# One two-run mask product per bank of transposed scores

## The chip, the cores and the metric

The kernel runs on one core of one Trainium2 chip. The metric is the device time of one execution in microseconds (us): median 1925.46 of three runs, 1924.97 to 1925.52.

## The reference

One transformer block on x of 2048 rows by 576, in float32: an adaptive layer norm, sliding-window attention with 32 heads of 18 channels, a second adaptive layer norm, a token mixer and an MLP. The change is in the attention, where row i sees row j if 0 <= i - j < 256:

```
h = _layernorm(x) * (1 + ca) + sa
scores = einsum("bhqd,bhkd->bhqk", q, k) * (Dh ** -0.5)
mask = (idx[:, None] - idx[None, :] >= 0) & (idx[:, None] - idx[None, :] < W)   # W = 256
p = softmax(where(mask, scores, -1e9))
o = einsum("bhqk,bhkd->bhqd", p, v)
x = x + ga * (o @ wo)
```

## The kernel before

The kernel has four stages in one program: projections to q, k and v (`qkv`), attention with the output projection woven in (`attention`), the mixer and the MLP. The order of all instructions is written out by hand: every step is entered with a due time by `at(t, f)`, `build` sorts the steps by that time and issues them, and each engine then works through its own list in that order. Buffers are given by tags; an instruction that takes a buffer waits until the last reader of the one before it is done.

**Units of attention.** The 2048 rows are four groups of 512 queries (g = 0 to 3). Within a group, `load(n)`, `qs`, `ks`, `mx` and `xm` run over n = 0 to 31, with g = n // 8. This text calls an n a head, though it holds four heads of the reference: two passes j = 0, 1, each over a pair of heads that lies side by side in the partitions. Scores are computed twice. First, `mx` makes them with queries in the partitions, in blocks of 64 queries, two blocks to a call (`bb` = 0 to 3); a product with the identity adds the mask (L450, L452), VectorE takes the maximum of each row (`red`, L460), TensorE transposes the maxima of a head (`mtr`, L468), ScalarE copies them (L472), and SP stores them as extra rows of the query tile (`mst`, L477). Second, two heads later, `xm` makes the scores again, transposed, with keys in the partitions and the maxima subtracted by the extra rows; `ex` (L522) takes their exponential on ScalarE, and `av` (L544) multiplies by the values.

**The transposed scores.** A pass has twelve blocks of 64 keys, b = -4 to 7 (group 0 has none below 0). Block b meets the queries `rng(b)`, at most 320 columns. `BANKS` (L479) packs the blocks into five PSUM banks of 512 columns: for example bank 0 holds block 0 at column 0 and block 5 at column 320. Banks take the tags s0 and s1 in turn, so a bank's first product waits for the exponential of two banks before. In each block the first 64 columns (the diagonal) and the last 64 (the window's far edge) may need a mask of 64 x 64, repeated for the two heads of the pass: `Mk[:, 1]` for the diagonal, `Mk[:, 0]` for the far edge. Each holds 0 or -1e30.

**The edited step.** `xm` issues the one to three score products of a bank (L492) and then its masks. It lists the columns that need a mask (`mk`), joins a far edge with the diagonal that begins just behind it into one run of 128 columns, and issues one product `identr` x `Mk` for each run (L517): the stationary operand is the identity, the moving operand the mask, and the result is added in PSUM. Where a bank has two runs of 128, it issues instead one product for the far edges of both and one for the diagonals of both, each with an output of two runs of 64 (L504 to L513). Every bank except number 4 so has two mask products, and bank 4 has one. The widths are 64 + 128 columns for banks 0 and 1 and 128 + 128 for banks 2 and 3 in groups 1 to 3; in group 0 they are 64 + 128, 64 + 64, 64 + 128, 64 + 128 and, for bank 4, 64. Both operands of every product are float32r, and each product has its own weight load.

**What shares the engines.** Between the steps of attention the schedule puts the output projection of finished rows (`wotile`): loads, transposes to T (L608, L610, copied at L615 to L618), the products (L629), the residual (L633), two layer norms (L116 to L122, L642, L643, L652) and stores. PSUM tags m0 and m1 belong to `mx`, s2 and s3 to the value products, the transposes and the projection. The query tiles have four buffers and the key tiles three; POOL makes the masked copies `QS` (L431) and `KS` (L438).

**Set-up.** `consts` clears `zb`, makes the identity and its float32r copy; `masks` clears `Mq` and `Mk`, fills them by four selections on POOL, and copies the lower 64 partitions to the upper 64 on VectorE (L103). `zb` serves only `warm`, which nothing calls.

Of the kernel before, what the change touches and what calls it, by code (L numbers as in the profile page):

```python
# [6 lines left out]

F32 = mybir.dt.float32
F32R = mybir.dt.float32r
BF16 = mybir.dt.bfloat16  # L10
# [8 lines left out]
P = 128  # L19
# [12 lines left out]
class Kern:  # L32
# [8 lines left out]
    def setup(self, stack):  # L41
        nc, tc = self.nc, self.tc
        self.ev = []
        self.cst = stack.enter_context(tc.tile_pool(name="cst", bufs=1))
        self.dr = stack.enter_context(tc.tile_pool(name="dr", bufs=1, space=DRAM))
        self.ps = stack.enter_context(tc.tile_pool(name="psU", bufs=1, space=PSUM))
        self.pools = {}
        c = self.cst
        self.zb = c.tile([P, P], BF16, name="zb")
        self.ident = c.tile([P, P], F32, name="ident")  # L50
        self.identr = c.tile([P, P], F32R, name="identr")
        self.gb = c.tile([P, D], F32, name="gb")
        self.mhalf = c.tile([P, 1], F32, name="mhalf")
        self.rowm = c.tile([P, 8], F32, name="rowm")
        self.Mq = c.tile([P, 2, 64], F32R, name="Mq")
        self.Mk = c.tile([P, 2, 64], F32R, name="Mk")
        self.md = c.tile([P, 10], F32, name="md")
        self.qd = [self.dr.tile([2, D, 512], F32, name=f"qd{g}") for g in range(4)]
        self.kd = [self.dr.tile([2, D, 768], F32, name=f"kd{g}") for g in range(4)]
        self.vd = [self.dr.tile([P, VW], F32, name=f"vd{t}") for t in range(NT)]  # L60
        self.od = [self.dr.tile([512, D], F32, name=f"od{g}") for g in range(4)]
        self.xp = [self.dr.tile([P, D], F32, name=f"xp{t}") for t in range(NT)]
        self.hbd = [self.dr.tile([P, D], F32, name=f"hbd{t}") for t in range(NT)]
        self.xnd = [self.dr.tile([P, D], F32, name=f"xnd{t}") for t in range(NT)]
        self.modd = {v: self.dr.tile([1, D], F32, name=f"modd{v}") for v in (2, 3, 4, 5)}

    def at(self, t, f, *a):
        self.ev.append((t, (lambda: f(*a)) if a else f))
# [14 lines left out]
    def consts(self):  # L83
        nc = self.nc
        g = nc.gpsimd
        g.memset(self.zb, 0.0)
        make_identity(nc, self.ident)
        nc.vector.tensor_copy(self.identr, self.ident)
        g.memset(self.mhalf, -0.5)

    def masks(self):
        nc = self.nc
        g = nc.gpsimd
        for M in (self.Mq, self.Mk):
            g.memset(M.bitcast(F32), 0.0)
        h = slice(0, 64)
        sel = lambda t, s, op, cm: g.affine_select(out=t, in_=t.bitcast(F32), pattern=[[s, 64]], compare_op=op, fill=NEG, base=0, channel_multiplier=cm)
        sel(self.Mq[h, 0], 1, ALU.is_gt, -1)
        sel(self.Mq[h, 1], -1, ALU.is_ge, 1)
        sel(self.Mk[h, 0], -1, ALU.is_gt, 1)  # L100
        sel(self.Mk[h, 1], 1, ALU.is_ge, -1)
        for M in (self.Mq, self.Mk):
            nc.vector.tensor_copy(M[64:128], M[0:64].bitcast(F32))  # L103
        m = self.rowm
        v = self.ident[:, 0:108].rearrange("p (u r d) -> p u r d", u=3, r=2)
        for r in range(2):
            nc.vector.tensor_reduce(out=m[:, r:r + 1], in_=v[:, :, r, :], axis=mybir.AxisListType.XY, op=ALU.add)
        nc.vector.tensor_tensor(out=m[:, 2:4], in0=m[:, 0:2], in1=self.ident[:, 108:110], op=ALU.add)
        nc.vector.tensor_reduce(out=m[:, 4:5], in_=self.ident[:, 108:110], axis=mybir.AxisListType.X, op=ALU.add)
# [17 lines left out]
    def qkv(self, T0, TB):  # L127
        nc, at, ps = self.nc, self.at, self.ps
# [189 lines left out]
        def vst(t):  # L318
            nc.sync.dma_start(self.vd[t], X["Vst"][t % 3])

        def warm(n):
            pw = ps.tile([P, 512], F32, tag="m0", name="pw")
            for _ in range(n):
                nc.tensor.matmul(pw, self.zb, self.zb.unsqueeze(1).to_broadcast([P, 4, P]), start=True, stop=True)

        at(-90, cond)
        for i in range(2):
            at(-89 + i, xload, i)
# [21 lines left out]
        for b in range(4):  # L350
# [7 lines left out]
            for i in range(4):  # L358
                t = 4 * b + i
# [16 lines left out]
            if b < 3:  # L376
                for i in range(4):
                    t = 4 * b + 4 + i
# [13 lines left out]
    def attention(self, t1, t2, TA, HU, LX=2.05):  # L392
        nc, at, ps = self.nc, self.at, self.ps
        X, M = {}, self.rowm
# [86 lines left out]
        def rng(b):  # L481
            return max(0, 64 * b), min(512, 64 * b + 320)

        def xm(n, j, k):
            g = n // 8
            px = X["px", n, j, k] = ps.tile([P, 512], F32, tag=f"s{(5 * j + k) % 2}", name=f"X{n}_{j}_{k}")
            Q, K = X["Q"][n % 4], X["ks", n, j]
            blocks = [x for x in BANKS[k] if g or x[0] >= 0]
            mk = []
            for i, (b, c) in enumerate(blocks):  # L490
                q0, q1 = rng(b)
                nc.tensor.matmul(px[:, c:c + q1 - q0], K[:, b + 4].rearrange("p r k -> p (r k)"), Q[:, j, q0:q1], start=(i == 0), stop=False)  # L492
                if b >= 0:
                    mk.append((c, 1))
                if b <= 3:
                    mk.append((c + q1 - q0 - 64, 0))
            mk.sort()
            runs = []
            for c, kind in mk:
                if kind == 1 and runs and runs[-1] == (c - 64, 64, 0):  # L500
                    runs[-1] = (c - 64, 128, 0)
                else:
                    runs.append((c, 64, kind))
            if len(runs) == 2 and runs[0][1] == 128 and runs[1][1] == 128:  # L504
                d = runs[1][0] - runs[0][0]
                c = runs[0][0]
                out = px[:, c:c + 128]
                o2 = px.rearrange("p (a b) -> p a b", b=64)
                a0, da = c // 64, d // 64
                for h in range(2):  # L510
                    pass
                full = [(o2[:, a0 + h:a0 + h + da + 1:da, :], self.Mk[:, h].unsqueeze(1).to_broadcast([P, 2, 64])) for h in range(2)]
                ops = full  # L513
            else:
                ops = [(px[:, c:c + w], self.Mk.rearrange("p a b -> p (a b)")[:, 64 * kind:64 * kind + w]) for c, w, kind in runs]
            for i, (o, mv) in enumerate(ops):
                nc.tensor.matmul(o, self.identr, mv, start=False, stop=(i == len(ops) - 1))  # L517

        def ex(n, j, k):
            lo = 0 if n >= 8 else (0, 192, 64, 128, 256)[k]  # L520
# [749 lines left out]
```

## Time and profile before

| | us |
|---|---|
| median of three runs | 1925.46 |
| the profiled execution | 1925.45 |
| its span | 1923.7 |
| PE busy | 1766.7 (92%) |
| VectorE busy | 1124.2 (58%) |
| POOL busy | 899.6 (47%) |
| ScalarE busy | 697.9 (36%) |
| mean granted TensorE clock | 0.956 |
| mask products of the transposed scores (L517), 576 of them, busy | 112.3 |
| first and last start of L517 | 252.3 and 734.3 |

PE is TensorE's matmuls, PEld its weight loads, DVE VectorE, ACT ScalarE, POOL GpSimd, SP the engine that issues most DMAs. In a row of a timeline stand the start in us from the beginning of the span, the duration, the engine, the line of the kernel, the operation, output <- inputs by the program's names, their shapes and the count of instructions in the row; in brackets the time that the engine had been idle before it, and what ended the wait. In a row of groups the numbers behind the bar are the busy time in us, the mean length of one in ns, and the idle time before. The granted clock is 1.00 at full speed; the rows show 1.00 and 0.50 and means of the two. The lengths of matmuls overlap, so that the starts tell more than the lengths.

### The profile page before, as it was taken

How to read it: one execution, taken by the hardware profiler on the slowest of the kernel's cores; microseconds unless marked ns; L12 is line 12 of the kernel's file. 1: busy time of each engine (PE TensorE's matmuls, PEld its weight loads, DVE VectorE, ACT ScalarE, POOL GpSimd, SP SyncE). 2: the span in 40 equal slices, each digit the busy share in tenths (PEclk: the TensorE clock that was granted, in tenths of full speed). 3: DMA queues.
4: the chain of work that ended last, by engine and by line, in shares of the span. 5: the costliest groups of instructions: out<-in, count | busy, mean ns of one | idle time of the engine just before them, and what ended most of it. 6: DMA issues, size and time to landing. Idle time of an engine off the chain costs nothing.

```text
span 1923.7 us, 34258 instructions
## 1 busy us (share of the span) xinstructions
PE 1766.7 (92%) x13752; PEld 1617.1 (84%) x13752; DVE 1124.2 (58%) x1840; ACT 697.9 (36%) x1194; POOL 899.6 (47%) x831
## 2 busy tenths in 40 slices
PE   7999998989999996787767999999998999999998
PEld 6788888889898986787756999999987899999997
DVE  4544335546665654666646666666676766666664
ACT  2222134434444444423314333333333333333331
POOL 4311364443544444244356556565552555555560
PEclk9999958899999998998887999999998999999999
DMA  4855552443635435444252211121214222222211
GB/s 149 305 178 176 166 144 78 116 123 114 177 110 172 123 93 177 149 154 154 73 175 82 58 58 58 58 58 58 59 56 135 60 58 60 60 61 60 59 46 49
DMA packets 156134, 206.75 MB, mean 107 GB/s; under 512 B 19012, under 2 KB 87620, under 8 KB 155400
## 3 DMA queue, kind: packets, MB, share of 16 engines
q1 hardware_dynamic: 155976, 204.57, 34.6%
q8 instruction: 108, 1.77, 0.4%
q14 instruction: 50, 0.41, 0.1%
HBM read 143.69 MB, written 60.56 MB: 106 GB/s over the span
## 4 chain that ended last, share of the span: by engine, by line
PE 57%; DVE 8%; DMA 3%; POOL 3%; ACT 3%; issue 3%; SPq 1%; DVEq 0%; POOLq 0%; ACTq 0%
PE d L1135 23%; PE av L544 3%; PE wo L629 3%; PE mx L448 2%; PE X L492 2%; PE w L856 2%; PE pg L807 1%; DVE W L994 1%; PE X L517 1%; DVE G L1112 1%; DMA wf<-in_B_w_dram 1%; PE mx L450 1%; PE u33P L1082 1%; PE u32P L1082 1%; PE u26P L1082 1%
## 5 line engine op out<-in xcount | busy, mean ns | idle before, releaser
L1135 PE MATMUL d<-W,G 128*128 128x288 f32 x3456 | 510.2, 298 | 12.5 <-DVE acc L1143 10.0
L1135 PEld LDWEIGHTS d<-W,G 128*128 128x128 f32 x3456 | 490.6, 190 | 35.2 <-DVE acc L1143 10.9
L1143 DVE TENSOR_TENSOR acc<-d,acc 128x576 f32<-128x576 f32 x288 | 216.7, 754 | 193.8 <-PE d L1135 189.5
L974 POOL TENSOR_TENSOR wf<-wf 128x384 f32<-128x384 f32 x140 | 144.9, 1056 | 351.9 <-DMA wf<-in_B_w_dram 351.9
L460 DVE TENSOR_REDUCE m<-mx 128x2 f32<-128x640 f32 x224 | 181.1, 817 | 172.9 <-PE mx L450 171.3
L522 ACT ACTIVATE P<-X 128x512 f32<-128x512 f32 (+4 forms) x320 | 182.0, 573 | 229.1 <-PE X L517 228.0
L448 PE MATMUL mx<-KD,QS 128*128 128x320 f32 (+4 forms) x512 | 168.5, 379 | 28.0 <-POOL QS L431 14.0
L492 PE MATMUL X<-QD,KS 128*128 128x64 f32 (+2 forms) x704 | 156.2, 313 | 1.2 <-ACT P L522 0.7
L431 POOL TENSOR_SCALAR QS<-QD,rowm 128x512 fp32r<-128x512 f32 x128 | 87.8, 699 | 144.0 <-DMA QD<-qd 89.8
L1112 DVE TENSOR_TENSOR G<-U,G 128x512 fp32r<-128x512 f32 x108 | 94.4, 874 | 99.0 <-ACT G L1105 99.0
L986 POOL TENSOR_TENSOR W<-wf,W 128x768 fp32r<-128x768 f32 x70 | 148.8, 2148 | 0.0
L1103 ACT ACTIVATE U<-U 128x512 f32<-128x512 f32 x108 | 68.4, 633 | 189.5 <-DVE U L1088 189.5
L448 PEld LDWEIGHTS mx<-KD,QS 128*128 128x128 f32 x512 | 104.0, 203 | 34.4 <-POOL QS L431 19.3
L1103 ACT ACTIVATE C<-C 128x512 f32<-128x512 f32 x36 | 22.7, 632 | 286.7 <-DVE C L1088 286.7
L278 PE MATMUL qk<-hT,Wqk 128*128 128x512 f32 x504 | 121.3, 402 | 0.0
L278 PEld LDWEIGHTS qk<-hT,Wqk 128*128 128x128 f32 x504 | 96.1, 192 | 24.3 <-issue 0.9
L517 PE MATMUL X<-Mk,identr 128*128 128x128 f32 (+1 forms) x576 | 112.3, 269 | 0.0
L492 PEld LDWEIGHTS X<-QD,KS 128*128 128x128 f32 x704 | 109.1, 199 | 2.5 <-ACT P L522 1.8
L1000 POOL TENSOR_TENSOR wf<-wf,gb 128x1152 f32<-128x1152 f32 x35 | 103.1, 2946 | 13.1 <-DMA wf<-in_B_w_dram 6.9
L438 POOL TENSOR_SCALAR KS<-KD,rowm 128x768 fp32r<-128x768 f32 (+1 forms) x128 | 108.5, 862 | 0.0
L980 ACT CAST W<-wf 128x1152 fp32r<-128x1152 f32 x70 | 90.2, 1319 | 47.2 <-DMA wf<-in_B_w_dram 34.6
L1015 POOL TENSOR_TENSOR W<-wf,W 128x1152 fp32r<-128x1152 f32 x35 | 96.3, 2752 | 13.8 <-ACT W L1009 13.8
(745 smaller groups left out, 3287.2 us busy)
## 6 DMA issues: line engine op xcount, KB each, us to landing
wf<-in_B_w_dram SPq DMA_DIRECT2D x35, 576.0 KB
wf<-in_B_w_dram SPq DMA_DIRECT2D x140, 128.0 KB
KD<-kd SPq DMA_DIRECT2D x72, 216.0 KB
QD<-qd SPq DMA_DIRECT2D x96, 144.0 KB
wf<-in_B_w_dram SPq DMA_DIRECT2D x140, 64.0 KB
qd<-qs SPq DMA_DIRECT2D x16, 512.0 KB
kd<-qs SPq DMA_DIRECT2D x16, 512.0 KB
vd<-Vst SPq DMA_DIRECT2D x16, 312.0 KB
```

What stands on the lines that cost most here:

```text
L278: nc.tensor.matmul(po, W[:, a, fs], H[:, c, :], start=(n == 0), stop=(n == 13))
L438: nc.gpsimd.tensor_scalar(t[:, b0:, r], src[:, b0:], M[:, 2 + r:3 + r], 0.0, op0=ALU.mult, op1=ALU.add)
L448: nc.tensor.matmul(pm[:, s, 320 - 64 * nb:320], lhs, K[:, j, 64 * (i + 5 - nb):64 * (i + 5)], start=True, stop=False)
L460: nc.vector.tensor_reduce(out=m[:, c:c + 2], in_=pm[:, :, 0:320], axis=mybir.AxisListType.X, op=ALU.max, negate=True)
L492: nc.tensor.matmul(px[:, c:c + q1 - q0], K[:, b + 4].rearrange("p r k -> p (r k)"), Q[:, j, q0:q1], start=(i == 0), stop=False)
L517: nc.tensor.matmul(o, self.identr, mv, start=False, stop=(i == len(ops) - 1))
L522: nc.scalar.activation(p[:, lo:], X["px", n, j, k][:, lo:], AF.Exp, scale=SCALE)
L974: nc.gpsimd.tensor_tensor(out=WF[:, o], in0=WF[:, a], in1=WF[:, b], op=ALU.subtract)
L986: eng.tensor_tensor(out=W[:, s0:s1, 3:5, :], in0=WF[:, 1 + s0:1 + s1, 0:2], in1=W[:, s0:s1, 0:2, :].bitcast(F32), op=ALU.subtract)
L1112: nc.vector.tensor_tensor(out=G[:, 1, ta, b], in0=up_b[jj, "gf", ta, b], in1=G[:, 0, ta, b].bitcast(F32), op=ALU.subtract)
L1135: nc.tensor.matmul(po, G[:, g, ta, b, ts], W[:, w, b, cs], start=(n == 0), stop=(n == 5))
L1143: nc.vector.tensor_tensor(out=a, in0=po, in1=a, op=ALU.add)
```

## The change

Every bank gets one mask product, whose output has two runs: each of 128 columns where there are two places to mask, with a run that needs only one mask of 64 widened by 64 columns of zeros (for bank 1 of group 0: two runs of 64). The score products, the exponentials and the order of all steps stay as they are. `Mk` grows from two to five pieces of 64 columns: far edge, diagonal, zero, far edge, diagonal. Its pieces 1 to 4 give "diagonal, zeros" and "far edge, diagonal" in one read; pieces 0 to 3 give "far edge, diagonal" and "zeros, far edge"; where both runs are "far edge, diagonal", pieces 0 and 1 are read twice. The zero piece is cleared by the memset of `Mk`, and one VectorE copy fills pieces 3 and 4. `zb`, its memset and the unused `warm` go.

```diff
-        self.zb = c.tile([P, P], BF16, name="zb")
...
-        self.Mk = c.tile([P, 2, 64], F32R, name="Mk")
+        self.Mk = c.tile([P, 5, 64], F32R, name="Mk")
...
-        g.memset(self.zb, 0.0)
...
+        nc.vector.tensor_copy(self.Mk[h, 3:5], self.Mk[h, 0:2].bitcast(F32))
         for M in (self.Mq, self.Mk):
             nc.vector.tensor_copy(M[64:128], M[0:64].bitcast(F32))
...
             for i, (b, c) in enumerate(blocks):
                 q0, q1 = rng(b)
                 nc.tensor.matmul(px[:, c:c + q1 - q0], K[:, b + 4].rearrange("p r k -> p (r k)"), Q[:, j, q0:q1], start=(i == 0), stop=False)
-                if b >= 0:
-                    mk.append((c, 1))
-                if b <= 3:
-                    mk.append((c + q1 - q0 - 64, 0))
...
-            for i, (o, mv) in enumerate(ops):
-                nc.tensor.matmul(o, self.identr, mv, start=False, stop=(i == len(ops) - 1))
+            o, mv = cut(px, g, k, self.Mk)
+            nc.tensor.matmul(o, self.identr, mv, start=False, stop=True)
+
+        def cut(t, g, k, M):
+            pairs = lambda c, st: AP(t[:, 0:1].tensor, t[:, c:c + 1].offset, [t[:, 0:1].ap[0], (st, 2), (1, 128)])
+            mk = lambda a, w: M[:, a:a + w].rearrange("p a b -> p (a b)")
+            split = lambda m: m.rearrange("p (a b) -> p a b", a=2)
+            both = mk(0, 2).unsqueeze(1).to_broadcast([P, 2, 128])
+            sz = split(mk(1, 4))
+            if g:
+                return ((pairs(0, 256), sz), (pairs(128, 256), split(mk(0, 4))), (pairs(0, 320), both), (pairs(64, 320), both), (t[:, 192:320], mk(0, 2)))[k]
+            return ((pairs(0, 256), sz), (pairs(192, 256)[:, :, 0:64], M[:, 1:4:2]), (pairs(64, 256), sz), (pairs(128, 256), sz), (t[:, 256:320], mk(1, 1)))[k]
```

More of the change, by code (lines that the diff above doesn't have):

```diff
@@ L5 @@
 from concourse import mybir
+from concourse.ap import AP
 from concourse.masks import make_identity
@@ L319, in vst @@
             nc.sync.dma_start(self.vd[t], X["Vst"][t % 3])
[L321 to L324, printed above, removed]
         at(-90, cond)
@@ L488, in xm @@
             blocks = [x for x in BANKS[k] if g or x[0] >= 0]
-            mk = []
             for i, (b, c) in enumerate(blocks):
@@ L492, in xm @@
                 nc.tensor.matmul(px[:, c:c + q1 - q0], K[:, b + 4].rearrange("p r k -> p (r k)"), Q[:, j, q0:q1], start=(i == 0), stop=False)
-                if b >= 0:
-                    mk.append((c, 1))
-                if b <= 3:
-                    mk.append((c + q1 - q0 - 64, 0))
[L497 to L515, printed above, removed]
-            for i, (o, mv) in enumerate(ops):
-                nc.tensor.matmul(o, self.identr, mv, start=False, stop=(i == len(ops) - 1))
+            o, mv = cut(px, g, k, self.Mk)
[9 more added lines that the diff above has]
+            return ((pairs(0, 256), sz), (pairs(192, 256)[:, :, 0:64], M[:, 1:4:2]), (pairs(64, 256), sz), (pairs(128, 256), sz), (t[:, 256:320], mk(1, 1)))[k]
         def ex(n, j, k):
```

## The prediction

> **What bounds the kernel now.** First the page for the span, then the groups of instructions kept apart by shape, to see what the edited line is made of.
>
> ```profile
> span 1923.7 us, 34258 instructions
> ```
>
> ```profile
> L450 PE MATMUL mx<-Mq,identr 128*128 128x128 f32 x448 | 102.2, 228 | 0.0
> L517 PE MATMUL X<-Mk,identr 128*128 128x128 f32 x384 | 91.8, 280 | 0.0
> L517 PE MATMUL X<-Mk,identr 128*128 128x64 f32 x192 | 44.6, 246 | 0.0
> ```
>
> There are 384 + 192 = 576 mask products, of 128 and of 64 columns. Their means (280 and 246 ns) are no price, since matmuls overlap. I need the pitch at which they follow each other. Third comes the busy time in stretches of the attention stage, each from one transpose of the maxima (L468) to the next: one head of mask work each.
>
> ```profile
> 251.60:266.60 15.00, 15.00 (x69) 15.00 (x68) 5.52 (x12) 6.38 (x13) 12.30 (x14) 0.50 0.56 147
> 266.60:281.60 15.00, 15.00 (x69) 15.00 (x68) 6.47 (x13) 6.30 (x13) 11.80 (x15) 0.50 0.21 61
> ...
> 351.10:363.50 12.40, 8.95 (x67) 8.86 (x68) 6.45 (x8) 5.17 (x11) 2.95 (x5) 0.89 0.63 168
> 507.70:520.40 12.70, 11.71 (x89) 11.23 (x89) 9.94 (x17) 6.25 (x11) 5.08 (x10) 1.00 0.59 165
> 520.40:538.90 18.50, 17.82 (x311) 16.97 (x310) 8.94 (x16) 8.20 (x16) 9.32 (x12) 1.00 0.37 108
> ```
>
> The columns are the stretch, its length, then PE, PEld, DVE, ACT and POOL busy, the granted clock, DMA share and GB/s. TensorE leads everywhere, but not in the same way. In the first two stretches it is never idle, at a clock of 0.50. In the third it is idle for 12.40 - 8.95 = 3.45 us. In the fourth VectorE has 9.94 us of work in 12.70. So one price will not do for the whole stage: I first find what a product costs, and then, head by head, whether that time is on the path.
>
> **Price of one product.** The pitch is read from the starts of the weight loads. At clock 1.00:
>
> ```profile
> 506.22 0.30 PEld L492 LDWEIGHTS X<-QD,KS 128*128 128x128 f32 x2
> 506.45 0.19 PEld L517 LDWEIGHTS X<-Mk,identr 128*128 128x128 f32 x1
> 506.57 0.19 PEld L448 LDWEIGHTS mx<-KD,QS 128*128 128x128 f32 x1
> ```
>
> ```profile
> 509.83 0.30 PEld L517 LDWEIGHTS X<-Mk,identr 128*128 128x128 f32 x2
> 510.05 0.19 PEld L448 LDWEIGHTS mx<-KD,QS 128*128 128x128 f32 x1
> ```
>
> ```profile
> 511.41 0.30 PEld L517 LDWEIGHTS X<-Mk,identr 128*128 128x128 f32 x2
> 511.63 0.19 PEld L448 LDWEIGHTS mx<-KD,QS 128*128 128x128 f32 x1
> ```
>
> By the program, the pair at 509.83 is bank 0 (64 and 128 columns) and the pair at 511.41 is bank 2 (128 and 128). Both take 0.22 us until the next load, 0.11 a product, whatever the width: a narrow product is paid by its weight load, not by its columns. The two loads at 506.22 are the score products of bank 4, 256 columns each. While the second of them streams, the loads go from 506.45 to 506.57: a slot of 0.12 us. A merged mask product has 256 columns, so a merge turns 0.22 into 0.12 and saves 0.10 us. At half clock:
>
> ```profile
> 277.01 0.54 PEld L517 LDWEIGHTS X<-Mk,identr 128*128 128x128 f32 x2
> 277.43 0.33 PEld L448 LDWEIGHTS mx<-KD,QS 128*128 128x128 f32 x1
> ```
>
> ```profile
> 280.47 0.33 PEld L517 LDWEIGHTS X<-Mk,identr 128*128 128x128 f32 x1
> 280.69 0.33 PEld L448 LDWEIGHTS mx<-KD,QS 128*128 128x128 f32 x1
> ```
>
> Two mask products take 0.42 there and the slot over bank 4's 256 columns 0.22: a merge saves 0.20 us.
>
> An output of two runs is not new. L450 writes two runs of 64 columns, 256 apart, and stands in the trace as one matmul of 128 columns. An output of two runs of 128 is not in the trace. Its slot lies between 0.11 (no dearer than a narrow product) and 0.22 (two runs paid like two products, no saving). I take 0.12, the row with the same number of columns.
>
> **How many.** Of the five banks of each pass over a pair of heads, four had two mask products and get one; bank 4 had one and keeps it. With 64 passes, two to each of the 32 heads counted here, 256 products and 256 loads go and 320 stay. The columns grow from 1024 to 1152 a pass in groups 1 to 3 (48 passes) and from 768 to 960 in group 0 (16 passes), by 48 x 128 + 16 x 192 = 9216 in all. If every merge were on the path, 16 at half clock would bring 3.2 us and 240 others 24.0: 27.2 us.
>
> **Heads 0 and 1** (251.6 to 281.6). PE is busy 15.00 us of 15.00 in both, so all of it is kept: 16 x 0.20 = **3.2 us**. A head shrinks to 13.4 us, and POOL, next in line with 12.30, still fits.
>
> **Heads 2 to 9.** They come in pairs, one with the value products (L544) and one without. The second kind, from four views in order of time:
>
> ```profile
> 351.16 0.28 PE L468 MATMUL mt<-ident,m 128*16 128x128 f32 x1 [0.17 <-DVE m L460]
> ```
>
> ```profile
> 353.02 0.50 SPq L423 DMA_DIRECT2D QD<-qd  x1
> ```
>
> ```profile
> 360.71 1.36 POOL L431 TENSOR_SCALAR QS<-QD,rowm 128x512 fp32r<-128x512 f32 x2 [9.45 <-DMA QD<-qd]
> ```
>
> ```profile
> 362.56 0.61 PE L448 MATMUL mx<-KD,QS 128*128 128x320 f32 x1 [3.40 <-POOL QS L431]
> ```
>
> L468 starts a chain. Its result lets SP store the maxima, and behind that store, in queue order, stand the loads for the head after next (353.02). POOL waits for them until 360.71, and PE has its queries at 362.56, 11.4 us after L468. All eight merges of the head lie between: PE arrives 0.8 us earlier and waits 4.2 us in place of 3.4. Nothing is kept. In the head with value products I count six of eight as kept, one lost to a reduction that has to free a bank and one to an exponential that does. Four such heads give 4 x 6 x 0.10 = 2.4, and 0.4 more because their bank 0 still runs at half clock: **2.8 us**.
>
> **Heads 10 to 29** are ten pairs alike. The one without value products, on VectorE and then on TensorE:
>
> ```profile
> 510.82 0.83 DVE L460 TENSOR_REDUCE m<-mx 128x2 f32<-128x640 f32 x1 [2.42 <-PE mx L450]
> ...
> 514.56 0.83 DVE L460 TENSOR_REDUCE m<-mx 128x2 f32<-128x640 f32 x1 [0.15 <-PE mx L450]
> ...
> 518.88 2.44 DVE L460 TENSOR_REDUCE m<-mx 128x2 f32<-128x640 f32 x3
> ```
>
> ```profile
> 518.05 0.42 PE L448 MATMUL mx<-KD,QS 128*128 128x320 f32 x1 [0.35 <-DVE m L460]
> ...
> 519.76 0.38 PE L448 MATMUL mx<-KD,QS 128*128 128x320 f32 x1 [0.62 <-POOL c3rs L119]
> ```
>
> From 510.82 to past 520 VectorE's one wait for another engine is 0.15 us: reductions with a layer norm between them. Each pair of L448 needs the reduction of two pairs before, whose buffer it takes, and PE waits for it at 518.05 and 519.76. (The second row names POOL. The first of the three reductions that begin at 518.88 ends near 519.7, a third of 2.44 later, and that is when PE starts.) The seven merges from 510.6 to 520 therefore only lengthen these waits. Bank 0 at 509.83 lies ahead and is kept: one of eight. The head with value products has ScalarE in the way:
>
> ```profile
> 527.10 0.60 ACT L522 ACTIVATE P<-X 128x512 f32<-128x512 f32 x1 [5.26 <-PE X L517]
> ...
> 529.33 1.07 ACT L549 COPY avs<-av 128x512 f32<-128x512 f32 x2
> ```
>
> ```profile
> 534.47 0.80 PE L629 MATMUL wo<-Wo,T 128*128 128x288 f32 x4 [0.29 <-DVE T L617]
> ```
>
> It is full from bank 1's exponential at 527.10 to the end of the copies at 530.4, and the transposes of those copies come next on PE, so banks 2 and 3 are lost. The casts of T hold the projection at 534.47, and the bank 2 that lies over them is lost. Five of eight are kept. A pair keeps six of sixteen: 10 x 6 x 0.10 = **6.0 us**.
>
> **Heads 30 and 31** (after 709) have no score pairs left, and ScalarE's exponentials, 0.60 each as above, pace most banks. I count five merges kept, one at half clock: **0.6 us**.
>
> **Set-up.** One more VectorE copy goes ahead of the statistics of the first tiles, and POOL has one memset less and a longer one:
>
> ```profile
> 9.08 0.21 DVE L103 CAST Mk<-Mk 64x128 fp32r<-64x128 f32 x1
> ...
> 13.76 0.46 DVE L116 BATCH_NORM_STATS2 a3st<-x 128x6 f32<-128x288 f32 x1 [1.04 <-DMA x<-in_A_x_dram]
> ```
>
> A copy of that size takes 0.21 us, and 1.04 us of waiting for the fourth tile hides it; without that cover it costs 0.2 us.
>
> **Sum.** 3.2 + 2.8 + 6.0 + 0.6 = 12.6 us off the profiled execution's own 1925.45 (span 1923.7 and 1.75 around it; the median of the runs is 1925.46): **1912.8 us**. More than half of the 27.2 goes into waits that are there already. Two merges a pair more or fewer are 2 us, and as much again is open in heads 2 to 9 and 30 to 31: its own range is 1909 to 1917.
>
> **The rivals.** (a) *Columns pace TensorE.* If the pitch were the columns' own at 0.12/256 = 0.47 ns each, removing loads would bring nothing and 9216 columns would cost 4.3 us: 1929.8, slower. It decides where a load takes less time than its columns stream; against it, 64 + 128 columns take the same 0.22 us as 128 + 128. Slots above 0.24 us for two runs of 128 would end on this side too. The Trainium skill ("TensorE: Matmul & The Clock Gate", Back-to-back issue gap) prices a lone warm product at N/2.4 + 2.5 ns, by which 9216 columns more and 256 products fewer come to 3.8 - 0.6 = 3.2 us slower; the trace's 0.22 us for both pairs does not agree with it. Chance 0.04.
>
> (b) *The waits take everything at full clock.* Only the first 3.2 us stay: 1922.3. For it speaks that PE waits in every pair already; against it, that in 520.4 to 538.9 no other engine is busy for even 10 of the 18.50 us. 0.06. That the two runs are issued as two products after all (1925.5) gets 0.02; L450 speaks against.
>
> (c) *The chains move with PE*, because exponentials and reductions start earlier too, and nearly all is kept: 1899. Against it stand the 11.4 us and VectorE's ten full microseconds. 0.08.
>
> (d) *The clock comes back early.* In 251.6 to 281.6 it is granted at 0.50 although PE never idles. Merged, the same work streams more columns in less time. If that releases the clock near 260, the two heads fall from 13.4 to the chain's 11.4 us, up to 4 us more: 1909. The same page's Part 1 lets some 3.4 us of sustained activity release the clock; by that rule these heads would run at full clock already, and the two rows of 0.50 do not agree. 0.14.
>
> **How the numbers follow.** Forecast 0.66, (d) 0.14, (c) 0.08, (b) with its pieces 0.08, (a) 0.04. The range holds the forecast's own and (d), and reaches part of the way to (b) and (c): 1904 to 1919.5. A measurement of this kernel can tell about 0.2%, 3.9 us, from no change. Faster: 0.66 + 0.14 + 0.08 = 0.88. Within: 0.08. Slower: 0.04.
>
> **What would show it.** L517 with 320 products and a slot of 0.12 us over each merged one; heads 0 and 1 of 13.4 us; the wait at 362.56 grown to about 4.2 us, those at 518.05 and 519.76 by 0.7 together; pairs of heads 0.6 us shorter than 12.70 + 18.50. I am wrong if the waits do not grow, or if a merged product's slot is near 0.22.

## The result, and the profile after

The changed kernel takes 1911.23 us, median of five runs (1907.75 to 1917.38), beside 1925.46 for the kernel before (1923.16 to 1928.7, five runs): a ratio of 0.993, with a 95% interval from 0.9907 to 0.9954. The forecast was 1912.8 us. The profiled execution is the fastest of the five, 1907.75 us, so its stages add up to more than the medians' 14.2 us. First the head of its page, and the edited line by shape.

```profile
span 1906.0 us, 33746 instructions
```

```profile
L488 PE MATMUL X<-Mk,identr 128*128 128x256 f32 x240 | 79.0, 329 | 0.0
L488 PEld LDWEIGHTS X<-Mk,identr 128*128 128x128 f32 x320 | 62.0, 194 | 0.0
```

L488 is the mask product (before: L517). It has 320 weight loads, 256 fewer, and 240 of its products are 256 columns wide. Lines have moved up: score product L492 to L486, `mx` L448 and L450 to L443 and L445, `red` L460 to L455, `mtr` L468 to L463, `ex` L522 to L503, `av` L544 to L525, `qs` L431 to L426, the projection's products L629 to L610. Next TensorE's weight loads around one merged product at full clock.

```profile
503.25 0.19 PEld L488 LDWEIGHTS X<-Mk,identr 128*128 128x128 f32 x1
503.36 0.19 PEld L443 LDWEIGHTS mx<-KD,QS 128*128 128x128 f32 x1
503.48 0.19 PEld L445 LDWEIGHTS mx<-Mq,identr 128*128 128x128 f32 x1
```

The loads are 0.11 and 0.12 us apart: the second interval is the one in which the 256 columns with two runs stream. Two runs cost no more than one. Then the stretches between transposes of the maxima that the prediction showed, with the same columns.

```profile
256.35:268.84 12.49, 10.28 (x62) 9.69 (x61) 5.52 (x12) 6.20 (x13) 10.93 (x13) 0.77 0.68 186
268.84:280.76 11.92, 10.50 (x61) 9.88 (x60) 6.14 (x15) 6.20 (x13) 10.13 (x12) 0.77 0.27 76
349.05:361.53 12.48, 8.53 (x59) 8.16 (x60) 6.48 (x8) 5.16 (x11) 3.70 (x6) 0.92 0.65 165
499.69:512.30 12.61, 11.12 (x81) 10.47 (x82) 9.89 (x17) 6.14 (x11) 5.06 (x10) 1.00 0.60 168
512.30:530.50 18.20, 17.35 (x303) 16.25 (x302) 8.96 (x16) 8.17 (x16) 9.24 (x12) 1.00 0.38 108
```

Heads 0 and 1 went from 15.00 us each to 12.49 and 11.92, and the clock in them from 0.50 to 0.77. The third stretch lost 0.42 us of matmuls (8.95 to 8.53) and took 12.48 us in place of 12.40. The fourth and fifth are shorter by 0.1 and 0.3 us. What TensorE waits for in them, in order of time:

```profile
265.47 0.44 PE L486 MATMUL X<-QD,KS 128*128 128x320 f32 x2 [0.87 <-ACT P L503]
267.96 0.42 PE L443 MATMUL mx<-KD,QS 128*128 128x64 f32 x1 [1.19 <-POOL QS L426]
```

```profile
360.54 0.60 PE L443 MATMUL mx<-KD,QS 128*128 128x320 f32 x1 [3.95 <-POOL QS L426]
```

```profile
505.69 0.39 PE L443 MATMUL mx<-KD,QS 128*128 128x320 f32 x1 [0.24 <-DVE m L455]
509.91 0.41 PE L443 MATMUL mx<-KD,QS 128*128 128x320 f32 x1 [0.63 <-DVE m L455]
511.62 0.38 PE L443 MATMUL mx<-KD,QS 128*128 128x320 f32 x1 [0.62 <-POOL c3rs L119]
526.14 2.14 PE L610 MATMUL wo<-Wo,T 128*128 128x288 f32 x14 [0.44 <-DVE T L598]
```

In heads 0 and 1 TensorE, never idle before, now waits for an exponential and for POOL. The wait for the queries grew from 3.40 to 3.95 us. In the pair at full clock the first wait for a maximum is new (0.24), the second grew from 0.35 to 0.63, the third stayed at 0.62, and the projection waits 0.44 where it waited 0.29. One more loss is a short one: the mask products of bank 0 just ahead of the value products, before and after.

```profile
520.77 0.30 PEld L517 LDWEIGHTS X<-Mk,identr 128*128 128x128 f32 x2
521.14 0.18 PEld L544 LDWEIGHTS av<-P,V 64*32 64x32 f32 x16
```

```profile
512.62 0.19 PEld L488 LDWEIGHTS X<-Mk,identr 128*128 128x128 f32 x1
512.96 0.18 PEld L525 LDWEIGHTS av<-P,V 64*32 64x32 f32 x16 [0.15 <-ACT ms L467]
```

Two products took 0.37 us until the next load (520.77 to 521.14), one takes 0.34 (512.62 to 512.96): this merge saves 0.03 us.

The whole span, cut at the starts of the transposes of the maxima (us, worked out from those starts; "again" is a second series of the changed kernel, below, whose profiled execution is the slowest of its six):

| stage | before | after | again |
|---|---|---|---|
| to head 0 (two transposes) | 251.6 | 256.3 | 255.4 |
| heads 0 and 1 | 30.0 | 24.4 | 25.4 |
| heads 2 to 9 | 111.4 | 108.1 | 109.4 |
| heads 10 to 29 | 316.1 | 306.8 | 309.1 |
| the rest, heads 30 and 31 in it | 1214.6 | 1210.4 | 1214.9 |
| span | 1923.7 | 1906.0 | 1914.2 |

The attention heads give 5.5 + 3.3 + 9.3 = 18.1 us, or 4.6 + 2.0 + 7.0 = 13.6 by the second series. The first and last stages, in which the change has next to nothing to do, differ by up to 4.6 us between the two executions of one kernel: no story is built on them. Heads 2 to 9 need the same caution, as the experiments' profiles show further down.

### The profile page after: what moved, and what is told of

Read it like the earlier page. It is cut to its first block, busy times and chain, and to the rows that moved or that the text cites. A ratio compares the mean times of both kernels' runs of the same rounds, so it can differ in the third digit from the quotient of the medians.

```text
span 1906.0 us, 33746 instructions
## 1 busy us (share of the span) xinstructions
PE 1735.2 (91%) x13496; PEld 1581.5 (83%) x13496; DVE 1127.5 (59%) x1841; ACT 696.4 (37%) x1194; POOL 898.7 (47%) x830
## 4 chain that ended last, share of the span: by engine, by line
PE 57%; DVE 8%; POOL 3%; DMA 3%; issue 3%; ACT 3%; SPq 1%; DVEq 0%; POOLq 0%; ACTq 0%
PE d L1116 23%; PE av L525 3%; PE wo L610 2%; PE pg L788 2%; PE w L837 2%; PE mx L443 2%; PE X L486 2%; DVE W L975 1%; DVE m L455 1%; DMA wf<-in_B_w_dram 1%; PE X L488 1%; PE u2P L1063 1%; PE u33P L1063 1%; PE u27P L1063 1%; PE u26P L1063 1%
## 5 line engine op out<-in xcount | busy, mean ns | idle before, releaser
L455 DVE TENSOR_REDUCE m<-mx 128x2 f32<-128x640 f32 x224 | 181.1, 817 | 156.4 <-PE mx L445 154.1
L503 ACT ACTIVATE P<-X 128x512 f32<-128x512 f32 (+4 forms) x320 | 180.4, 573 | 207.3 <-PE X L488 204.8
L443 PE MATMUL mx<-KD,QS 128*128 128x320 f32 (+4 forms) x512 | 155.9, 355 | 37.2 <-POOL QS L426 20.6
L426 POOL TENSOR_SCALAR QS<-QD,rowm 128x512 fp32r<-128x512 f32 x128 | 87.4, 696 | 142.8 <-DMA QD<-qd 68.2
L486 PE MATMUL X<-QD,KS 128*128 128x64 f32 (+2 forms) x704 | 150.1, 305 | 3.1 <-ACT P L503 2.7
L443 PEld LDWEIGHTS mx<-KD,QS 128*128 128x128 f32 x512 | 100.9, 197 | 44.9 <-POOL QS L426 21.9
L486 PEld LDWEIGHTS X<-QD,KS 128*128 128x128 f32 x704 | 106.0, 193 | 9.3 <-ACT P L503 6.3
L445 PE MATMUL mx<-Mq,identr 128*128 128x128 f32 x448 | 100.9, 225 | 0.0
```

Source lines behind the costliest of these rows:

```text
L443: nc.tensor.matmul(pm[:, s, 320 - 64 * nb:320], lhs, K[:, j, 64 * (i + 5 - nb):64 * (i + 5)], start=True, stop=False)
L445: nc.tensor.matmul(pm[:, s, 0:320].rearrange("p (a b) -> p a b", b=64)[:, 0::4, :], self.identr, self.Mq, start=False, stop=True)
L455: nc.vector.tensor_reduce(out=m[:, c:c + 2], in_=pm[:, :, 0:320], axis=mybir.AxisListType.X, op=ALU.max, negate=True)
L503: nc.scalar.activation(p[:, lo:], X["px", n, j, k][:, lo:], AF.Exp, scale=SCALE)
```

## The experiments

**The same kernel again, and its products cut in two.** The first has no edit, for the spread. The second issues each run of a merged product as a product of its own, with the wide runs, the zeros and the set-up as they are.

```diff
-            nc.tensor.matmul(o, self.identr, mv, start=False, stop=True)
+            if k < 4:
+                for r in range(2):
+                    nc.tensor.matmul(o[:, r], self.identr, mv[:, r], start=False, stop=(r == 1))
+            else:
+                nc.tensor.matmul(o, self.identr, mv, start=False, stop=True)
```

> The changed kernel once more, unaltered. The first profiled execution lost 4.6 us before the first mask product (first L463 at 245.33 us against 240.69 before) and gained 22 us after it. Theory: the early loss is the landing of the first DMAs, which differs from execution to execution, and not the set-up code; a second profile then shows the first L463 somewhere else, between 240 and 246 us, and again heads 0 and 1 of 12 to 13.4 us with the clock released in between. Rival: the longer set-up costs 4 us each time, and L463 starts at 245 again.

> The changed kernel with each run of a merged mask product issued as a product of its own: 576 products of mostly 128 columns, as many loads as before the change and as many columns as after it. Theory (the weight load is the price, 0.11 us a product up to 192 columns): the time of before, 1925 us within 4 us, heads 0 and 1 at 15.0 us and a clock of 0.50 in them. Rival (columns are the price): 4 us slower than before, near 1930. Rival (the gain came from elsewhere, the set-up or the smaller first pool): as fast as after, 1911.

Again: 1915.84 us, ratio 0.9938 (0.9922 to 0.9955) to 1927.12. The first transpose of the maxima starts at 243.92 us (before 240.69, in the first series 245.33), between 240 and 246 as expected, so the early loss is not the set-up's each time. In two pieces: 1925.75, ratio 0.9997 (0.9982 to 1.0012); its heads 0 and 1 take 29.97 us, as before. The gain hangs on the number of products, and with it of instructions. The zero columns and the set-up bring nothing and cost nothing that can be told.

**Merging in heads 0 and 1 alone, and everywhere else.** Where the condition does not hold, a bank gets two pieces as above.

```diff
-            if k < 4:
+            if not (n < 2 or k == 4):
```

The second kernel has `n >= 2` in place of `n < 2`.

> Merged products in heads 0 and 1 alone, 16 merges; all others as two products. Theory: these two heads shrink as in the changed kernel, by 3.2 us through the loads and by 2.4 more because the clock comes back, and the rest of the kernel stays as before: 1919 to 1922 us. If the clock of these heads is what decides the rest too, it comes near 1911; if the merges' price there is small, it stays at 1925.

> Merged products everywhere but in heads 0 and 1, 240 merges. Theory: heads 0 and 1 stay at 15.0 us and a clock of 0.50; heads 10 to 29 give 0.4 to 0.6 us a pair, heads 2 to 9 about 0.6 a pair: 9 us off, 1916 us. If all 240 were on the path it would be 1901.

All but two: 1917.6 us, ratio 0.9956 (0.9937 to 0.9975), as expected. The first two alone: 1929.08, ratio 1.0003 (0.9988 to 1.0018), a miss. In its profile the two heads did shrink:

```profile
253.16:266.44 13.28, 13.28 (x61) 13.28 (x60) 5.53 (x12) 6.31 (x13) 11.56 (x14) 0.50 0.61 171
266.44:278.71 12.27, 10.55 (x61) 9.87 (x61) 6.19 (x13) 6.20 (x13) 9.57 (x12) 0.78 0.27 74
```

Head 0 is 13.28 us with TensorE never idle at a clock of 0.50: that is the forecast's 13.4, without help from the clock. In head 1 the clock comes back. Together they save 4.4 us, and the timed runs do not show it. The profiled run is the shortest of its ten. In it the value products are about as long as before (the measure is given further down: 5.0 us over their undisturbed time, against 4.9). Where the other runs lost the 4.4 us stays open. The run with 240 merges settles rival (b): with waits that take everything at full clock it would have gained nothing, and its pairs of heads without a stall are 30.81 us, where they were 31.22.

**The loads a head earlier, with two products and with one.** To take away the wait for the queries, tiles get one more buffer and are loaded 1.6 heads ahead in place of 0.8. Room comes from `KS` (3 buffers for 4) and `P` (22 for 24). The same edit is made to both kernels.

```diff
-            X["Q"] = [a1([P, 2, 512], F32R, name=f"QD{i}") for i in range(4)]
-            X["K"] = [a1([P, 2, 768], F32R, name=f"KD{i}") for i in range(3)]
+            X["Q"] = [a1([P, 2, 512], F32R, name=f"QD{i}") for i in range(5)]
+            X["K"] = [a1([P, 2, 768], F32R, name=f"KD{i}") for i in range(4)]
...
-            at(max(t1 + .5 + n * .01, tm(n - 0.8)), load, n)
+            at(max(t1 + .5 + n * .01, tm(n - 1.6)), load, n)
```

> The kernel before the change with one more query tile and one more key tile, the loads of a head entered 0.8 of a head earlier, and, to make room, three masked key tiles in place of four and 22 buffers of exponentials in place of 24. Theory: the wait of 3.4 us at the end of each of heads 3, 5, 7 and 9 is the chain from the transposed maxima through SP's queue and the load, so it goes: heads 3, 5 and 7 fall from 11.1 to 12.4 us to 8 or 9, and with the gap the half clock behind it goes. Heads 2 to 9 fall from 111.4 to about 97, the kernel to 1912. Rival: POOL or the transfers themselves are the limit, and heads 2 to 9 stay above 108.

> The changed kernel with the same earlier loads. Theory: with the load's chain out of the way, the 32 merges of heads 3, 5, 7 and 9 are on the path too, so that heads 2 to 9 gain 4 to 6 us over the same kernel with two products, against 2 to 3.3 us with the late loads; the kernel comes to about 1896. Rival: the merges in these heads were not hidden by that chain, and the two kernels with early loads differ by no more than the two without.

With two products 1916.66 us, ratio 0.9945 (0.9926 to 0.9964); with one 1897.6, ratio 0.9859 (0.9827 to 0.9892). The second beats both kernels. The stretch of head 7 in each, two products first:

```profile
344.65:353.38 8.73, 8.55 (x68) 8.38 (x68) 6.45 (x9) 5.17 (x11) 6.26 (x9) 1.00 0.59 149
```

```profile
342.41:350.67 8.26, 8.12 (x60) 7.66 (x60) 6.54 (x9) 5.16 (x11) 6.26 (x9) 1.00 0.55 143
```

The wait of 3.40 us is gone, TensorE is busy nearly all through, and now the eight merges of the head are worth 0.47 us, where they were worth -0.1 (12.40 against 12.48). Heads 3 and 5 say the same: 8.76 to 8.31 and 8.66 to 8.19. So the wait had eaten them. But eight slots of 0.10 would be 0.8 us. Weight loads around bank 1, two products first, and ScalarE beside the second:

```profile
345.83 0.34 PEld L517 LDWEIGHTS X<-Mk,identr 128*128 128x128 f32 x2
346.11 0.30 PEld L492 LDWEIGHTS X<-QD,KS 128*128 128x128 f32 x2
```

```profile
343.48 0.19 PEld L488 LDWEIGHTS X<-Mk,identr 128*128 128x128 f32 x1
343.81 0.30 PEld L486 LDWEIGHTS X<-QD,KS 128*128 128x128 f32 x2
```

```profile
343.16 1.17 ACT L503 ACTIVATE P<-X 128x512 f32<-128x512 f32 x2 [0.18 <-PE X L488]
```

Two products took 0.28 us until bank 2's first load, one takes 0.33. Bank 2 needs the buffer of bank 0, whose exponential is the first of the two that begin at 343.16: by half of 1.17 it ends near 343.75, and the load follows at 343.81. So the exponentials take what bank 1's merges free, a wait that the prediction did not count in these heads.

Over heads 2 to 9 the two profiles differ by 0.5 us only (92.0 and 91.5), which misses the 4 to 6 expected. Head 8 takes 16.86 us with one product and 14.13 with two, and 1.9 of that is one stall of TensorE of the kind described below. The early loads with two products bring heads 2 to 9 from 111.4 to 92.0 us, but heads 10 to 29 get 2.3 us longer, the rest 7.0 and the start 3.5, so that 6.6 of the 19.4 us arrive in the profile (9.3 in the timed runs). I did not follow up where those go.

**VectorE made lighter.** One pass of L643 and the statistics of the third norm are left out and its result is replaced by a copy of `h`, so one output differs.

```diff
-            nc.vector.scalar_tensor_tensor(out=h, in0=h, scalar=rs, in1=X["sb"], op0=ALU.mult, op1=ALU.add)
...
-            X["s2", t] = self.stats(X["h", t], self.pool_("wo"), f"c{t}", True)
+            pass
...
-            nc.scalar.activation(xn, h, AF.Identity, scale=rs, bias=nb)
+            nc.scalar.copy(xn, h)
```

> The kernel before the change without the second half of the second layer norm's shift (L643), without the statistics of the third norm, and with a plain copy in its place on ScalarE: 1.9 us less on VectorE in each pair of heads from 10 to 29. Theory: VectorE is what makes PE wait twice in the head without value products (0.5 and 0.7 us), so a pair falls from 31.3 to about 30.2 us; heads 10 to 29 from 316 to 305. Rival: these waits belong to POOL or to the loads, and a pair stays at 31.3.

> The changed kernel with the same part left out. Theory: with VectorE lighter, the seven merges that only lengthened its waits are kept, at least in part: a pair falls by 0.8 to 1.2 us against the same kernel with two products, where it fell by 0.4 to 0.6 with VectorE full. Rival: the difference of a pair stays at 0.4 to 0.6, and it was not VectorE that took the merges.

1913.73 us with two products, ratio 0.9925 (0.9898 to 0.9952), and 1897.42 with one, ratio 0.9854 (0.982 to 0.9888). The first came as expected: heads 10 to 29 take 305.8 us in place of 316.1, so the work left out, most of it VectorE's, is on their path. From one to the other a pair of heads loses 0.80 us in the mean and 0.59 in the median, against 0.93 and 0.58 between the two full kernels; the shortest pairs are 29.89 and 28.54. The expectation of a clearly larger saving was not met. So how many merges VectorE alone takes is not settled. The comparison showed something else: most pairs of the changed kernel are alike to 0.01 us (30.80, 30.80, 30.80, 30.81), and those with two products are not (31.22, 31.21, 31.68, 31.35).

**Where the pairs differ: the value products.** In heads 10 to 29 the ten stretches of 416 instructions of `av` (208 products with their loads) take 4.74 us each when undisturbed. In the profile before they take up to 5.8 us at full clock, after nearly always 4.74. Two rows of one such stretch before, by its weight loads, then what the waits of those loads add up to from 395 to 700 us (us in total, times, longest), before and after:

```profile
646.53 2.96 PEld L544 LDWEIGHTS av<-P,V 64*32 64x32 f32 x137
650.48 1.22 PEld L544 LDWEIGHTS av<-P,V 64*32 64x32 f32 x47 [0.98 <-issue]
```

```profile
PEld av L544 <- issue: 3.2, 8, 1.0
```

```profile
PEld av L525 <- issue: 0.4, 1, 0.4
```

"issue" means that no other engine had to release it. The page's rows for the queue that carries instructions are, before and after:

```profile
q8 instruction: 108, 1.77, 0.4%
```

```profile
q8 instruction: 106, 1.74, 0.4%
```

1.77 MB in 108 packets are 16 KB each. TensorE has 27,813 records before, its sequencer's included, which are some 257 a packet. I numbered the records in order. In the twelve traces of this study with the loads where they were, 33 gaps of over 0.25 us stand inside value products at full clock after 395 us, and all 33 lie at a number that is 192 or 193 modulo 256. Position within the stretch matters as well: of 115 such places among the first 229 instructions none has a gap of over 0.25 us, of 87 from 230 on 31 have one, up to 1.98 us. The packets themselves are in the traces and bear this out: at each of these 31 places TensorE goes on 2.2 to 3.0 us after one of the 16 KB packets began, and 1.2 to 1.7 us after it was over, and there are only 106 to 108 packets in a whole run. A stretch runs through 416 instructions in 4.74 us, faster than anything else here; that the supply has less lead left the later in the stretch it meets the end of a packet's worth is how I read the rows, not shown by itself.

This is also why the changed kernel is spared. A pair of heads has 808 TensorE instructions before, 3 x 256 + 40, so the place moves 40 a pair and in ten pairs walks through the whole stretch. It has 776 after, 3 x 256 + 8: the place moves by 8, from 245 to 171, and after the first two pairs lies ahead of 230 in all. The Trainium skill ("Runtime: NRT & Kernel Launch", Instruction fetch mechanics) says that instructions are refilled in blocks of 16 KiB, 256 instructions, and that crossing a block is mostly hidden. The block agrees with the rows; that it is hidden does not, in this stream: some 3 us of 305.

**Merging in only half of the heads 10 to 29**: those with value products (n even), then those without (n odd). Both remove the same number of instructions.

```diff
+            if 10 <= n < 30 and n % 2 == 0 or k == 4:
```

> The merged product only in the ten heads among 10 to 29 that also hold value products; all other banks get their two runs as two products. Theory 1 (a merge is worth its slot where no wait takes it): in the profiles the ten pairs took 316.1 and 314.7 us with two products and 306.8 to 309.1 with one, and of that only some 0.30 us a pair were shorter slots in the heads with value products. So this alone should give about 312 (3 us off 315), with value products that still stall as before (their ten stretches together 3 to 5 us above the undisturbed 47.4). Theory 2 (the stalls of the value products come from the number of instructions that TensorE is fed with, and half the merges take half of the stalls away): 309 to 311, stretches 1 to 3 us above. Timed: 1922 or 1920 against some 1926.

> The merged product only in the ten heads among 10 to 29 without value products, where I had put nearly all merges into waits for VectorE. It removes as many instructions as the run before it. Theory 1: some 0.11 us a pair, so 314 to 315 us for the ten pairs, and value products that stall as with two products everywhere (3 to 5 us above 47.4): 1925 timed, no change that can be told. Theory 2: the stalls shrink as much as in the run before it, so 311 to 313 us for the pairs, 1922 timed; if all of them go although no value product is near a merged one, 310.

With value products 1926.36 us, ratio 0.9992 (0.9971 to 1.0013), without 1927.53, ratio 1.0 (0.9982 to 1.0017). In the profiles heads 10 to 29 take 310.9 and 319.2 us. The pairs without a stall are 30.93 and 31.15 us, against 31.22 with two products and 30.80 with one: about 0.3 for the heads with value products and about 0.1 for the others. Issue waits of the value products, with and without:

```profile
PEld av L529 <- issue: 1.7, 4, 0.5
```

```profile
PEld av L529 <- issue: 5.0, 10, 1.8
```

The two rows can't be compared as they stand: 1.9 of the 5.0 us are six gaps of 0.31 us in stretches at half clock, which are not at such places. At full clock the stretches are 2.1 and 3.3 us over their undisturbed time, while the profiles before and in two pieces, with the same places as each other, have 3.1 and 2.6. So this pair does not decide between the theories; the next one does better. Both kernels have 792 a pair, 3 x 256 + 24, which also walks through the stretch. The profiles are not typical either: the first is the shortest of its twelve runs, the second the longest but one. The timed runs show no gain in either half, where merging in all but two heads showed 0.44%. The interval of the first does not exclude its 3 us (it reaches down to 0.29%), but that the halves add up to the whole isn't shown.

**Moving the places on purpose.** Two kernels with small products of zeros, added into banks that are there: 48 of them once, in head 3, where TensorE waits anyway; then one beside each merged product, which brings the count back to 808 a pair.

```diff
+            for _ in range(6 if n == 3 and k < 4 else 0):
+                nc.tensor.matmul(px[0:32, 320:384], self.identr[:, 0:32], self.Mk[:, 2], start=False, stop=False)
```

The second kernel has `range(1 if k < 4 else 0)`.

> The changed kernel with 48 products of zeros (32 x 64 outputs, added to banks that are there) put once into head 3, where TensorE waits for its queries anyway. Counted over TensorE's stream (products and weight loads), every stall inside the value products in the ten traces so far began at an instruction whose number is 192 modulo 256, and only where that instruction was number 230 or later of the 416 of its value products; the instruction fetches move 16384 bytes at a time. In the changed kernel those instructions lie at 245, 237, 229 ... 171 in the stretches from head 10 on, 8 further ahead a pair of heads (776 instructions a pair, 3 x 256 + 8). 96 instructions more put them at 149 ... 75 and again at 405 ... 331. Theory 1 (supply of instructions): the ten stretches of value products rise from 0.5 to 2.4 us above the undisturbed ones to 2 to 5 us, and heads 10 to 29 from 307 to 309 us to 309.5 to 312, although nothing is changed in them. Theory 2 (the stalls came with the two products themselves): they stay at 0.5 to 2.4 and at 307 to 309. Timed between 1911 and 1917; the profile decides.

> The changed kernel with one product of zeros (32 x 64) beside each merged product, 256 in all, so that TensorE gets as many instructions as before: 808 for a pair of heads, with instruction 192 modulo 256 at the same places of the value products as before. The merged products and their wide outputs stay. Theory 1 (supply of instructions): the ten stretches of value products are 3 to 5.5 us above the undisturbed ones, as in the runs with two products, and heads 10 to 29 take 312 to 314 us in place of 307 to 309; some 0.03 to 0.05 us for each small product that no wait hides is in this. Theory 2: stretches 0.5 to 2.4 above, heads 10 to 29 at 308 to 310.5. Timed: 1918 to 1922 by theory 1, 1913 to 1916 by theory 2.

Once 48: 1915.5 us, ratio 0.9951 (0.9927 to 0.9975), not to be told from the changed kernel. The profile tells it: heads 10 to 29 take 312.8 us, and the value products are 5.8 us over their undisturbed time (4.2 of it in two stretches that lie partly at half clock), in heads in which nothing was edited. Both are a little above what theory 1 gave (312 and 5). By the second series, where 3.41 us of half clock made a stretch 1.48 us longer, the clock's part is an estimated 2.2, which leaves some 3.5 us of stalls; in the changed kernel's two profiles that is 0.5 and 0.

```profile
PEld av L527 <- issue: 4.1, 10, 1.6
```

```profile
457.72 4.45 PEld L527 LDWEIGHTS av<-P,V 64*32 64x32 f32 x195 [0.15 <-ACT ms L467]
462.55 0.18 PEld L527 LDWEIGHTS av<-P,V 64*32 64x32 f32 x13 [0.38 <-issue]
```

The stall has moved to the 390th instruction, where the shift puts it. At full clock the six stretches with places from 397 down to 348 are each 0.15 to 0.38 us over; the last two, with places at 339 and 331, are not, and their pairs are 30.31 us as in the changed kernel. Theory 1 holds. The count brought back: 1924.36, ratio 0.9978 (0.9959 to 0.9997), heads 10 to 29 of 314.7 us, value products 2.9 over, a little under the 3 to 5.5 expected. But 1.9 of it lies in one stretch at half clock, and so it does before; the rest is 1.0 here and 3.1 before, at the same places. So the places say where stalls can come, not how long they get in one execution.

```profile
PEld av L527 <- issue: 1.5, 5, 0.5
```

Its pairs without a stall are 31.31 us, 0.5 longer than those of the changed kernel: most of what it lost is the price of the small products themselves. So it says less about the supply than its neighbour, and more about the first step of the prediction: a product of 64 columns with a load of 32 costs a pair as much as a mask product does.

## Why the prediction was right, step by step

**The price of a product** held: 0.12 us for two runs of 128 (503.36 to 503.48), 256 products gone, and with the same columns in two pieces no gain at all. Rival (a), that columns set the pace, is refuted by that run. The rival that two runs are issued as two products falls by the rows: 320 loads, and 240 products of 256 columns. Rival (c), that nearly all is kept (1899), lies outside the runs of the changed kernel, 1907.75 to 1917.38.

**Heads 0 and 1** were the term that was sized too low: 3.2 forecast, 5.5 and 4.6 in the two profiles. The step itself was right, as head 0 of 13.28 us at half clock shows. What came on top is rival (d), to which I had given 0.14: in all seven profiles with merging in these heads the clock came back within them, with 11.0 to 18.7 us left at half speed; in all seven without, it stayed at 0.50 for the whole 29.97 us. Whether the 4 to 5 us reach the timed runs is not settled: merging there alone showed nothing.

**Heads 2 to 9**: 2.8 forecast, 3.3 and 2.0 between the profiles, but that confirms nothing. Five profiles with two products in these heads have 111.4, 106.9, 111.8, 105.7 and 109.2 us there, three with one have 108.1, 109.4 and 105.2: the spread of one kind is larger than the forecast, and what the merges bring stays open. That the heads without value products keep nothing was right (12.40 to 12.48), and for the reason given: with the loads early the same merges are worth 0.47. The wait came out at 3.95 us, not 4.2, since TensorE arrived 0.46 us earlier and not 0.8 (7.54 us into the head, where it was 8.00); the exponentials behind bank 1 take part of it, as shown with the early loads.

**Heads 10 to 29**: 6.0 forecast, 9.3 and 7.0 measured (307.3 us with merges in all but two heads, 314.7 and 316.9 in the runs with two products here, agree). Here the step "five of eight are kept" failed. Pairs without a stall went from 31.22 to 30.80 us, so four of sixteen merges are kept, not six: one of eight in the head without value products, as forecast (12.72 to 12.61), and three of eight in the other (18.50 to 18.20). One more went to the projection's wait, and most of another to the value products behind the first bank 0 (0.03 us saved in place of 0.10). The growth of the waits for the maxima was 0.52 us (0.24 new, 0.28 more at the second), not 0.7. So slots gave some 4.1 us. The other 5 us of the first profile have two sources. The value products were 4.9 us over their undisturbed time before, 0.5 after (2.4 by the second series). But 1.9 of the 4.9 lies in the first stretch, which ran 4.3 of its 6.5 us at half clock, and the second series' 2.4 lie in stretches at half clock too. Stalls at full clock went from 3.1 us to 0.5 (to 0 by the second series). About 2.3 us of the first profile's gain are that first pair's half clock, 5.4 us of it before and none after; by the second series the clock gave nothing. The traces of before had the stalls in them, and the prediction did not see them. That forecast and result are near each other here is luck: one error covers another.

**Set-up, heads 30 and 31**: 0 and 0.6 are far below the 4.6 us by which these stages differ between executions. The sum came within 1.6 us of the first series' median and 3.0 of the second's. Shorter slots, the mechanism of the forecast, are shown for some 7.5 us of the profiles' 13.6 to 18.1 (3.4 by head 0 at half clock twice over, and 4.1), where the forecast had 12.6 by them. The rest is the clock in the first heads and in one pair, the place of instruction blocks in the value products, and heads 2 to 9, which stay open. So the time was right in part by luck.

## What to carry to other kernels

Price a TensorE edit by the distance of weight loads in the trace, then ask head by head, or loop by loop, which wait ends last: here four of sixteen removed products counted in heads 10 to 29, and in a head that waited for its queries none, until an earlier load took that wait away. The two changes together gave 0.9859 (0.9827 to 0.9892); the product of the two alone, 0.988, lies in that interval, so only the rows show that one helps the other. When an edit changes the number of TensorE instructions in a loop with a dense run of short products, look at that number modulo 256 before crediting the edit with the time, and shift the count once without any other change as a control.

## What the runs showed of the hardware that was not expected

TensorE's stream stalls for up to 1.98 us at one instruction in 256 where a run of products is dense, 0.0114 us an instruction, and has already lasted for some 230 of them, and goes on 2.2 to 3.0 us after a packet of instructions began. It need not be inside the run: two such stalls, at 194 modulo 256, begin 1.8 and 0.8 us behind the end of one, the first with early loads and one product, the second with merges in heads without value products.

```profile
358.45 0.19 PEld L443 LDWEIGHTS mx<-KD,QS 128*128 128x128 f32 x1 [1.88 <-issue]
```

```profile
627.37 0.34 PEld L492 LDWEIGHTS X<-Mk,identr 128*128 128x128 f32 x2 [0.74 <-issue]
```

The granted clock changes in steps of 3.4 us: 289 of the 303 stretches at half clock in the fourteen traces are a multiple of that long. TensorE's being busy does not suffice to raise it: before, it had work in 34.10 of the 34.10 us from 251.6 to 285.7 and stayed at 0.50 in all of them with two products, and the clock came back with one product over more columns. It also came back where each merged product had a small one beside it, as many instructions as before, so the number of instructions is not what holds it down. The Trainium skill ("TensorE: Matmul & The Clock Gate", Part 1) has a free-running window of 3413 ns, which agrees with the steps; that a busy window releases the clock does not agree with these 34 us. That it is the density of columns that decides is argued, not shown.
